# One attention wave for batch 0, the second product of block 0 by weight groups, spreads of four pairs and output stores on another queue

## The chip, the cores and the metric

The kernel runs on one core of one Trainium2 chip. The metric is the device time of a whole execution in microseconds (us). The profile's span, from the first to the last instruction, is about 2 us shorter than that time.

## The reference

```python
def _attn_ref(q, k, v):                       # B, H, S, D = 8, 8, 576, 64
    theta = np.pi / 2.0 * np.arange(S) / S
    phi = lambda x: concat([relu(x) * cos(theta), relu(x) * sin(theta)])
    q_p, k_p = phi(q), phi(k)
    kv = einsum('bhsf,bhsd->bhfd', k_p, v)
    z = sum(k_p, axis=2)
    return einsum(q_p, kv) / (einsum(q_p, z) + 1e-06)
# x = attention output as 4608 rows of 512; then, with w_in (512 x 2048) and w_out (2048 x 512)
def _moe_ref(x, w_in, w_out):
    h = x @ w_in
    return (h * sigmoid(1.702 * h)) @ w_out
```
The kernel keeps x in on-chip memory, transposed, and never writes it out.

## The kernel before

Nine blocks of 512 rows each go through the two products. Step n of a block is one chunk of the first product (`mm1`, steps 0 to 15) or a quarter of an output tile of the second (`mm2`, steps 16 to 31). The attention of batch i+1 is cut into small units that are laid between the steps of block i. Only batch 0's attention has nothing to hide behind.

```python
    def mm1(i, fc):                      # 4 products, then gelu on ACT into one of 18 buffers
        hps = hps_tile()                 # 2 PSUM buffers
        ...
        nc.scalar.activation(g, hps, AF.Gelu_apprx_sigmoid)
    def mm2(i, t, part):                 # 4 of the 16 products of output tile t
        if part == 0:
            cur[t] = yps_tile()          # 2 PSUM buffers
        ...
        if part == 3:
            ysb = ypool.tile([128, d_model], F32, name="ysb")     # 3 buffers
            nc.scalar.copy(ysb, yps)
            ...
            nc.scalar.dma_start(out=out[...], in_=ysb[...])       # stores issued by ACT
    # batch 0, before the blocks
    for jh in range(2):                  # the whole path twice, two pairs of heads each time
        ...                              # scale v (DVE, some on ACT)
        unit_kv(0, 2 * jh); unit_kv(0, 2 * jh + 1)
        unit_den(0, 2 * jh, 2 * jh + 2)  # denominators, reciprocal, split into three parts
        warmup(4)                        # products on a zero tile, results unused
        for j in (2 * jh, 2 * jh + 1):
            unit_spread(0, j)            # 4 small products (32 rows) and 2 ACT copies
            unit_num(0, j)               # numerator products, times spread, into x
    # between the steps of block i, for batch b = i + 1
    for j in range(NP):
        at(k0 + 22 + 2 * j, unit_spread, b, j)
        at(min(32, k0 + 23 + 2 * j), unit_num, b, j)
```

w_in is requested when batch 0's v has landed, batch 1 when w_in has, and w_out when batch 1's v has.

## Time and profile before

| | before |
|---|---|
| median time | 353.48 us (three runs when the prediction was made, 352.16 to 353.84) |
| span of the profile, mean granted clock | 350.0 us, 0.963 |
| TensorE busy | 326.8 us, 93% |
| VectorE (DVE), ScalarE (ACT) busy | 157.1 and 138.9 us |
| first w_in product of block 0 / block 1 / block 2 | 38.07 / 77.28 / 112.01 us |

The table of busy time by stage, in the prediction below, is the one to read: where TensorE does not keep up with its own work (block 0's start, and the 0.93 us at some block ends) something else sets the time. Everywhere else only fewer TensorE microseconds help.

### The profile page before, as it was taken

The numbers are of one execution on the slowest core, as the hardware profiler recorded it, in microseconds if no ns is written. First come the engines' busy times: TensorE is split into PE (matmuls) and PEld (weight loads), VectorE is DVE, ScalarE is ACT, GpSimd is POOL, SyncE is SP. The second block draws the span as 40 slices with busy tenths as digits, with TensorE's granted clock in tenths as the row PEclk, the third lists the DMA queues.
The fourth block names the chain that finished last, engine by engine and source line by source line (L and its number), as shares of the span: only waits on it lengthen the run. The fifth ranks groups of instructions, "written<-read, shape, count | busy, mean of one in ns | idle before, by whom it ended". The sixth has DMA issues, their size and how long they took to land.

```text
span 350.0 us, 4868 instructions
## 1 busy us (share of the span) xinstructions
PE 326.8 (93%) x1861; PEld 158.4 (45%) x1896; DVE 157.1 (45%) x388; ACT 138.9 (40%) x259; POOL 16.4 (5%) x45
## 2 busy tenths in 40 slices
PE   8477899999999899999998999999989999999994
PEld 3242345444544454445444544454535444444441
DVE  5657734447635644574457444654474420000000
ACT  3321553146322642264226423642364236424611
POOL 8400500000000000000000000000000000000000
PEclk9755899999999999999999999999999999999998
DMA  7999999913951893059215921501140120011022
GB/s 219 245 190 348 331 229 283 315 65 69 326 139 31 121 350 94 30 118 367 72 41 137 346 56 55 99 0 62 31 97 3 30 62 30 0 75 46 0 61 61
DMA packets 62217, 45.80 MB, mean 131 GB/s; under 512 B 28914, under 2 KB 57586, under 8 KB 62194
## 3 DMA queue, kind: packets, MB, share of 16 engines
q1 hardware_dynamic: 52466, 31.86, 32.1%
q10 hardware_dynamic: 5504, 9.44, 9.7%
q0 software_dynamic: 4224, 4.19, 7.3%
q8 instruction: 15, 0.25, 0.3%
q14 instruction: 8, 0.07, 0.1%
HBM read 36.70 MB, written 9.44 MB: 132 GB/s over the span
## 4 chain that ended last, share of the span: by engine, by line
PE 83%; DVE 9%; ACT 3%; ACTq 2%; issue 2%; DVEq 0%
PE hps L320 34%; PE yps L348 30%; PE at L259 5%; PE at L310 5%; PE at L298 3%; DVE den L285 3%; PE hps L72 2%; PE at L276 2%; ACTq L354 2%; PE att L208 1%; DVE vt L252 1%; ACT ysb L352 1%; DVE den L289 1%; DVE den L287 1%; DVE qT L212 1%
## 5 line engine op out<-in xcount | busy, mean ns | idle before, releaser
L348 PE MATMUL yps<-w_out_sb,g 128*128 128x512 bf16 x552 | 135.3, 380 | 1.7 <-issue 0.8
L320 PE MATMUL hps<-xT,w_in_sb 128*128 128x512 bf16 x566 | 129.4, 382 | 4.8 <-ACT g L323 4.1
L323 ACT ACTIVATE g<-hps 128x512 bf16<-128x512 f32 x144 | 85.5, 597 | 49.9 <-PE hps L320 49.5
L320 PEld LDWEIGHTS <-w_in_sb 128*128 128x128 bf16 x576 | 56.4, 98 | 72.3 <-issue 8.5
L348 PEld LDWEIGHTS <-g 128*128 128x128 bf16 x576 | 53.5, 98 | 54.5
L352 ACT COPY ysb<-yps 128x512 f32<-128x512 f32 x36 | 21.1, 586 | 77.1 <-PE yps L348 72.2
L312 DVE TENSOR_TENSOR xT<-at,invb 128x288 bf16<-128x288 f32 x64 | 26.7, 453 | 54.3 <-PE at L310 52.3
L302 ACT COPY invb<-at 128x288 f32<-128x288 f32 x64 | 22.6, 402 | 70.1 <-PE at L298 69.6
L262 DVE TENSOR_TENSOR zs<-at,mask_z 128x256 bf16<-128x256 f32 x32 | 13.6, 425 | 33.5 <-PE at L259 33.5
L259 PE MATMUL at<-vt,kr 128*128 128x258 bf16 x160 | 25.5, 289 | 2.7 <-DVE vt L252 1.3
L225 DVE TENSOR_TENSOR qT<-qTr,trig 128x576 bf16<-128x576 bf16 x48 | 18.2, 452 | 15.3 <-DMA qTr<-qn 15.3
L310 PE MATMUL at<-qT,kvs 128*128 128x288 bf16 x128 | 22.5, 297 | 0.7 <-ACT invb L302 0.5
L259 PEld LDWEIGHTS <-kr 128*128 128x128 bf16 x160 | 16.0, 101 | 13.3 <-issue 2.6
L252 DVE TENSOR_SCALAR vt<-vf,cosw 128x512 bf16<-128x512 f32 (+3 forms) x45 | 19.6, 447 | 0.0
L252 DVE TENSOR_SCALAR vt<-vf,sinw 128x512 bf16<-128x512 f32 (+3 forms) x39 | 18.1, 463 | 0.0
L298 PE MATMUL at<-den,sel 32*128 32x144 bf16 x128 | 14.1, 229 | 3.3 <-DVE den L289 3.1
L310 PEld LDWEIGHTS <-kvs 128*128 128x128 bf16 x128 | 12.6, 100 | 10.1 <-issue 1.4
L298 PEld LDWEIGHTS <-sel 32*128 32x128 bf16 x128 | 8.0, 94 | 17.9 <-issue 13.3
L265 DVE TENSOR_TENSOR kvs<-at,mask_n 128x256 bf16<-128x256 f32 x32 | 13.3, 414 | 0.0
L72 PE MATMUL hps<-warm 128*128 128x512 bf16 x31 | 11.3, 535 | 1.5 <-DVE halfpi L115 1.2
L212 DVE TENSOR_TENSOR qT<-att,trig 128x576 bf16<-128x576 bf16 x16 | 6.5, 450 | 9.3 <-PE att L208 9.3
L196 DVE TENSOR_SCALAR qn<-qf 128x1024 bf16<-128x1024 f32 x15 | 10.4, 696 | 0.0
(56 smaller groups left out, 95.9 us busy)
## 6 DMA issues: line engine op xcount, KB each, us to landing
qf<-in_q_dram SPq DMA_DIRECT2D x7, 1024.0 KB, 5.9
kf<-in_k_dram SPq DMA_DIRECT2D x7, 1024.0 KB, 8.4
vf<-in_v_dram SPq DMA_DIRECT2D x7, 1024.0 KB, 9.1
out_dram<-ysb ACTq DMA_DIRECT2D x40, 128.0 KB, 2.4
out_dram<-ysb ACTq DMA_DIRECT2D x16, 256.0 KB, 2.3
w_in_sb<-in_moe_w_in_dram POOLq DMA_DIRECT2D x4, 512.0 KB, 8.7
w_out_sb<-in_moe_w_out_dram POOLq DMA_DIRECT2D x4, 512.0 KB, 13.6
qf<-in_q_dram SPq DMA_DIRECT2D x2, 512.0 KB, 5.0
```

Source lines behind the costliest of these rows:

```text
L72: nc.tensor.matmul(wps, warm[:, 0:128], warm, start=True, stop=True)
L225: nc.vector.tensor_tensor(s["qT"][:, j, cs, :], s["qTr"][:, j, :], trig[:, cs, :], op=MUL)
L252: nc.vector.tensor_scalar(o, i, w, None, op0=MUL)
L259: nc.tensor.matmul(kv_ps[:, 0:VW], kr[:, c, j, :], vt[:, c, j, :], start=(c == 0), stop=(c == 4))
L298: nc.tensor.matmul(bps[:, ds(g2 * SEG, SEG)], sel[32 * j:32 * j + 32, 2 * hf + g2].rearrange("p hh d -> p (hh d)"), s["comb"][32 * j:32 * ...
L302: nc.scalar.copy(invb, bps[:, 0:HF])
L310: nc.tensor.matmul(num_ps[:, 0:HF], s["kvs"][j][:, cs, :], s["qT"][:, j, cs, ds(hf * HF, HF)], start=(cs == 0), stop=(cs == 1))
L312: nc.vector.tensor_tensor(xT[:, j, ds(b * S + hf * HF, HF)], num_ps[:, 0:HF], s["invb"][j, hf], op=MUL)
L320: nc.tensor.matmul(hps, w_in_sb[:, kc, ds(fc * 128, 128)], xT[:, kc, ds(i * TB, TB)], start=(kc == 0), stop=(kc == NP - 1))
L323: nc.scalar.activation(g, hps, AF.Gelu_apprx_sigmoid)
L348: nc.tensor.matmul(yps, gT[fc][:, ds(t * 128, 128)], w_out_sb[:, fc, :], start=(fc == 0), stop=(fc == FC - 1))
L352: nc.scalar.copy(ysb, yps)
```

## The change

The intent: run batch 0's attention path once instead of twice; hide late w_out groups; use four row groups of the array at once; take the stores off ACT.

```diff
-    SRC = (("qf", q), ("kf", k), ("vf", v))
+    SRC = (("qf", q), ("vf", v), ("kf", k))
 ...
-            cur[t] = yps_tile()
+            cur[t] = hps_tile() if i == 0 and t >= 2 else yps_tile()
 ...
-                nc.scalar.dma_start(out=out[...], in_=ysb[...])
+                nc.sync.dma_start(out=out[...], in_=ysb[...])
 ...
+    def unit_spread(b, hf):
+        bps = [at_tile() for _ in range(NP)]
+        for g2 in range(2):
+            for j in range(NP):
+                nc.tensor.matmul(bps[j][...], sel[32 * j:32 * j + 32, ...], s["comb"][32 * j:32 * j + 32, :], ...)
+        for j in range(NP):
+            nc.scalar.copy(invb, bps[j][:, 0:HF])
 ...
-    for jh in range(2):  ... (the two half waves)
+    warmup(14)
+    for j in range(NP):
+        unit_kv(0, j)
+    unit_den(0)
+    warmup(10)
+    for hf in range(2):
+        unit_spread(0, hf)
+        for j in range(NP):
+            unit_num(0, j, hf)
 ...
+            for hf in range(2):
+                n = k1 + 9 + 7 * hf
+                at(min(32, n), unit_spread, b, hf)
+                for j in range(NP):
+                    at(min(32, n + 3 + j // 2), unit_num, b, j, hf)
 ...
+            elif i == 0:
+                mm2(i, n % 4, (n - FC) // 4)
```
(Left out, among others: the attention's four PSUM buffers now serve transposes too, batch 0's kv results are copied by ACT, in blocks 1 to 6 the DMA transposes and the next loads are issued in the other order, the denominator has one more step before the spread, and w_in and w_out are asked for when the last load, now k, has landed.) In block 0 the loads of batch 2, called at step 28, now come on the SP queue behind the first output store, because both are on SP.

More of the change, by code (lines that the diff above doesn't have):

```diff
@@ L63, in yps_tile, with at_tile @@
         return ps.tile([128, TB], F32, name="yps", bufs=2)
-    def at_tile(dt=F32):
-        return ps.tile([128, TB if dt == F32 else 2 * TB], dt, name="at" if dt == F32 else "att",
-                       bufs=3 if dt == F32 else 1)
+    def at_tile():
+        return ps.tile([128, TB], F32, name="at", bufs=4)
     def warmup(n):
@@ L102 @@
     load_part(s0["qf"], q, 0, 4, 8)
+    load_part(s0["vf"], v, 0, 0, 8)
+    load_tail(s0["vf"], v, 0)
+    load_tail(s0["kf"], k, 0)
     load_part(s0["kf"], k, 0, 0, 4)
-    load_tail(s0["kf"], k, 0)
-    load_part(s0["vf"], v, 0, 0, 4)
-    load_tail(s0["vf"], v, 0)
     load_part(s0["kf"], k, 0, 4, 8)
-    load_part(s0["vf"], v, 0, 4, 8)
     tmp = ExitStack()
@@ L201, in prep_q_tail, with transpose_pe @@
                                 op0=MAX)
-    def transpose_pe(b, j):
+    def transpose_pe(b, j, step):
         s = state[b]
-        tp = at_tile(BF16)
-        for c in range(5):
-            np_ = 128 if c < 4 else 64
-            nc.tensor.transpose(tp[:, c * 128:c * 128 + np_],
-                                s["qn"][:np_, c, 2 * j:2 * j + 2, :].rearrange("p h d -> p (h d)"),
-                                ident[:np_, :np_])
+        if step == 0:
+            s["tp", j] = tp = at_tile().bitcast(BF16)
+            for c in range(5):
+                np_ = 128 if c < 4 else 64
+                nc.tensor.transpose(tp[:, c * 128:c * 128 + np_],
+                                    s["qn"][:np_, c, 2 * j:2 * j + 2, :].rearrange("p h d -> p (h d)"),
+                                    ident[:np_, :np_])
+            return
         for cs in range(2):
-            nc.vector.tensor_tensor(s["qT"][:, j, cs, :], tp[:, 0:S], trig[:, cs, :], op=MUL)
+            nc.vector.tensor_tensor(s["qT"][:, j, cs, :], s["tp", j][:, 0:S], trig[:, cs, :], op=MUL)
     def transpose_dma(b):
@@ L259, in unit_kv @@
             nc.tensor.matmul(kv_ps[:, 0:VW], kr[:, c, j, :], vt[:, c, j, :], start=(c == 0), stop=(c == 4))
-        kvs = two.tile([128, 2, 128], BF16, name="kvs", bufs=4)
+        if b == 0:
+            kvs = s["kvs0"][j]
+        else:
+            kvs = two.tile([128, 2, 128], BF16, name="kvs", bufs=4)
         zs = two.tile([128, 2, NSEG, 32], BF16, name="zs", bufs=4)
@@ L264, in unit_kv, with unit_den @@
             mask_z.rearrange("p s hh t r -> p s (hh t r)").unsqueeze(1).to_broadcast([128, 2, NSEG, 32]), op=MUL)
-        nc.vector.tensor_tensor(kvs, kv_ps[:, 0:256].rearrange("p (cs e) -> p cs e", cs=2), mask_n, op=MUL)
+        kv3 = kv_ps[:, 0:256].rearrange("p (cs e) -> p cs e", cs=2)
+        if b == 0:
+            for r in (slice(0, 64), slice(64, 128)):
+                nc.scalar.copy(kvs[r, :, r], kv3[r, :, r])
+        else:
+            nc.vector.tensor_tensor(kvs, kv3, mask_n, op=MUL)
         s.setdefault("kvs", []).append(kvs)
         s.setdefault("zs", []).append(zs)
-    def unit_den(b, j0=0, j1=NP):
+    def unit_den(b):
         s = state[b]
@@ L274, in unit_den @@
             for cs in range(2):
-                for j in range(j0, j1):
+                for j in range(NP):
                     nc.tensor.matmul(den_ps[32 * j:32 * j + 32, 0:SEG], s["zs"][j][:, cs, g, :],
@@ L278, in unit_den @@
                                      start=(g == 0 and cs == 0), stop=(g == NSEG - 1 and cs == 1))
-        r = slice(32 * j0, 32 * j1)
-        if j0 == 0:
-            s["d"] = [two.tile([128, SEG], dt, name=f"den{n}", bufs=1)
-                      for n, dt in enumerate((F32, F32, BF16, F32, BF16, BF16))]
-        den, inv, p0, d1, p1, comb = s["d"]
-        nc.vector.tensor_scalar(den[r], den_ps[r, 0:SEG], 1e-6, None, op0=ADD)
-        nc.vector.reciprocal(inv[r], den[r])
-        nc.vector.tensor_copy(p0[r], inv[r])
@@ L287, in unit_den @@
-        nc.vector.scalar_tensor_tensor(d1[r], p0[r], part1[r], inv[r], op0=MUL, op1=ADD)
-        nc.vector.tensor_copy(p1[r], d1[r])
-        nc.vector.scalar_tensor_tensor(comb[r], p1[r], part2[r], d1[r], op0=MUL, op1=ADD)
+        den, inv, p0, d1, p1, comb = [two.tile([128, SEG], dt, name=f"den{n}", bufs=1)
+                                      for n, dt in enumerate((F32, F32, BF16, F32, BF16, BF16))]
+        nc.vector.tensor_scalar(den, den_ps[:, 0:SEG], 1e-6, None, op0=ADD)
+        nc.vector.reciprocal(inv, den)
@@ L290, in unit_den @@
+        nc.vector.tensor_copy(p0, inv)
+        nc.vector.scalar_tensor_tensor(d1, p0, part1, inv, op0=MUL, op1=ADD)
+        nc.vector.tensor_copy(p1, d1)
+        nc.vector.scalar_tensor_tensor(comb, p1, part2, d1, op0=MUL, op1=ADD)
         s["comb"] = comb
-    def unit_spread(b, j, on=None):
+        s["invb"] = {}
+    def unit_spread(b, hf):
         s = state[b]
-        s.setdefault("invb", {})
-        for hf in range(2):
-            bps = at_tile()
-            for g2 in range(2):
-                nc.tensor.matmul(bps[:, ds(g2 * SEG, SEG)],
+        bps = [at_tile() for _ in range(NP)]
+        for g2 in range(2):
+            for j in range(NP):
+                nc.tensor.matmul(bps[j][:, ds(g2 * SEG, SEG)],
@@ L299, in unit_spread, with unit_num @@
                                  sel[32 * j:32 * j + 32, 2 * hf + g2].rearrange("p hh d -> p (hh d)"),
                                  s["comb"][32 * j:32 * j + 32, :], start=True, stop=True)
-            invb = two.tile([128, HF], F32, name="invb", bufs=4)
-            nc.scalar.copy(invb, bps[:, 0:HF])
+        for j in range(NP):
+            invb = two.tile([128, HF], F32, name="invb", bufs=8)
+            nc.scalar.copy(invb, bps[j][:, 0:HF])
             s["invb"][j, hf] = invb
-    def unit_num(b, j):
+    def unit_num(b, j, hf):
@@ L306, in unit_num @@
         s = state[b]
-        for hf in range(2):
-            num_ps = at_tile()
-            for cs in range(2):
-                nc.tensor.matmul(num_ps[:, 0:HF], s["kvs"][j][:, cs, :], s["qT"][:, j, cs, ds(hf * HF, HF)],
-                                 start=(cs == 0), stop=(cs == 1))
-            nc.vector.tensor_tensor(xT[:, j, ds(b * S + hf * HF, HF)], num_ps[:, 0:HF], s["invb"][j, hf], op=MUL)
-    gT = {}
+        num_ps = at_tile()
+        for cs in range(2):
+            nc.tensor.matmul(num_ps[:, 0:HF], s["kvs"][j][:, cs, :], s["qT"][:, j, cs, ds(hf * HF, HF)],
+                             start=(cs == 0), stop=(cs == 1))
@@ L317, in mm1, with mm1_part, gelu @@
+        nc.vector.tensor_tensor(xT[:, j, ds(b * S + hf * HF, HF)], num_ps[:, 0:HF], s["invb"][j, hf], op=MUL)
+    gT = {}
+    def mm1_part(hps, i, fc, kc):
+        nc.tensor.matmul(hps, w_in_sb[:, kc, ds(fc * 128, 128)], xT[:, kc, ds(i * TB, TB)],
+                         start=(kc == 0), stop=(kc == NP - 1))
+    def gelu(hps, fc):
+        g = gpool.tile([128, TB], BF16, name="g")
+        nc.scalar.activation(g, hps, AF.Gelu_apprx_sigmoid)
+        gT[fc] = g
     def mm1(i, fc):
@@ L319, in mm1 @@
         for kc in range(NP):
-            nc.tensor.matmul(hps, w_in_sb[:, kc, ds(fc * 128, 128)], xT[:, kc, ds(i * TB, TB)],
-                             start=(kc == 0), stop=(kc == NP - 1))
-        g = gpool.tile([128, TB], BF16, name="g")
-        nc.scalar.activation(g, hps, AF.Gelu_apprx_sigmoid)
-        gT[fc] = g
+            mm1_part(hps, i, fc, kc)
+        gelu(hps, fc)
     def pieces(m):
@@ L353, in mm2 @@
             for (p0, n, row, step) in pieces(i * 4 + t):
-                nc.scalar.dma_start(out=out[row:row + (n - 1) * step + 1:step, :], in_=ysb[p0:p0 + n, :])
+                nc.sync.dma_start(out=out[row:row + (n - 1) * step + 1:step, :], in_=ysb[p0:p0 + n, :])
     junk = const.tile([1, 16], F32)
     AC = nc.scalar
+    s0["kvs0"] = [two.tile([128, 2, 128], BF16, name="kvs", bufs=4) for _ in range(NP)]
+    for t in s0["kvs0"]:
+        nc.gpsimd.memset(t, 0.0)
     prep_new(0)
@@ L362 @@
     prep_q(0, 4, 8, AC)
-    warmup(24)
-    transpose_pe(0, 0)
-    transpose_pe(0, 1)
+    warmup(26)
+    for j in range(NP):
+        transpose_pe(0, j, 0)
+    for j in range(2):
+        transpose_pe(0, j, 1)
+    for c in range(5):
+        prep_v(0, c, 0)
+        prep_v(0, c, 1, on=AC)
+    for j in range(2, NP):
+        transpose_pe(0, j, 1)
     prep_k(0, 0, 4, AC)
     prep_k_tail(0)
-    transpose_pe(0, 2)
-    transpose_pe(0, 3)
-    nc.gpsimd.tensor_copy(junk[:, 0:1], s0["vf"][0:1, 0:1])
+    prep_k(0, 4, 8)
+    nc.gpsimd.tensor_copy(junk[:, 0:1], s0["kf"][0:1, 0:1])
     for g in range(4):
@@ L375 @@
     load_all(1)
-    nc.gpsimd.tensor_copy(junk[:, 1:2], state[1]["vf"][0:1, 0:1])
+    nc.gpsimd.tensor_copy(junk[:, 1:2], state[1]["kf"][0:1, 0:1])
     for g in range(4):
         nc.gpsimd.dma_start(out=w_out_sb[:, ts(g, 4), :], in_=wout_r[:, ts(g, 4), :])
-    for jh in range(2):
-        if jh == 1:
-            prep_k(0, 4, 8, AC)
-        for c in range(5):
-            prep_v(0, c, 0, 4 * jh, 4 * jh + 4)
-            prep_v(0, c, 1, 4 * jh, 4 * jh + 4, AC if c < 3 else None)
-        unit_kv(0, 2 * jh)
-        unit_kv(0, 2 * jh + 1)
-        unit_den(0, 2 * jh, 2 * jh + 2)
-        warmup(4)
-        for j in (2 * jh, 2 * jh + 1):
-            unit_spread(0, j)
-            unit_num(0, j)
+    warmup(14)
[5 more added lines that the diff above has]
+        unit_spread(0, hf)
+        for j in range(NP):
+            unit_num(0, j, hf)
     for i in range(NBLK):
@@ L401 @@
         if b < B:
-            if i > 0:
-                at(0, load_all, b + 1) if b + 1 < B else None
-            k0 = 4 if i == 0 else 0
+            k0 = 6 if i == 0 else 0
             at(k0, prep_new, b)
@@ L407 @@
             at(k0, prep_q_tail, b)
-            at(k0 + 1, prep_q, b, 4, 8)
+            at(k0, prep_q, b, 4, 8)
             if i == 0:
                 for j in range(NP):
-                    at(k0 + 5 + j, transpose_pe, b, j)
-            else:
-                at(k0 + 1, transpose_dma, b)
-            at(k0 + 2, prep_k, b, 0, 4)
-            at(k0 + 2, prep_k_tail, b)
-            at(k0 + 3, prep_k, b, 4, 8)
+                    at(k0 + 2 + j, transpose_pe, b, j, 0)
+                    at(k0 + 2 + j, transpose_pe, b, j, 1)
+            else:
+                at(k0, transpose_dma, b)
+                if b + 1 < B:
+                    at(k0 + 1, load_all, b + 1)
             for c in range(5):
                 for cs in range(2):
-                    at(k0 + 4 + c, prep_v, b, c, cs)
+                    at(k0 + 2 + c, prep_v, b, c, cs)
+            at(k0 + 7, prep_k, b, 0, 4)
+            at(k0 + 7, prep_k_tail, b)
+            at(k0 + 8, prep_k, b, 4, 8)
             if i > 0:
@@ L422 @@
                     at(k0 + 9 + j, prep_trig, b, j)
+            k1 = 17 if i == 0 else 12
             for j in range(NP):
-                at(k0 + 14 + j, unit_kv, b, j)
-            at(k0 + 19, unit_den, b)
-            for j in range(NP):
-                at(k0 + 22 + 2 * j, unit_spread, b, j)
-                at(min(32, k0 + 23 + 2 * j), unit_num, b, j)
+                at(k1 + j, unit_kv, b, j)
+            at(k1 + 5, unit_den, b)
+            for hf in range(2):
+                n = k1 + 9 + 7 * hf
+                at(min(32, n), unit_spread, b, hf)
+                for j in range(NP):
+                    at(min(32, n + 3 + j // 2), unit_num, b, j, hf)
             if i == 0 and b + 1 < B:
```

## The prediction

> **What bounds the kernel now.** I read the page's slices first, then busy time by stage, then the chain, then the order of time at the places where a stage ends.
>
> ```profile
> PE   8477899999999899999998999999989999999994
> ...
> PEclk9755899999999999999999999999999999999998
> ...
> DMA  7999999913951893059215921501140120011022
> ```
> (The page's slices, 8.75 us each.) TensorE is busy everywhere except in slices 2 to 4, where it also runs at half clock, while the DMA engines are full until about 70 us. So there are two regimes: a start limited by loads and by a serial chain, and a long stretch that is nothing but TensorE work.
>
> ```profile
> core 0: us, PE busy (x) PEld busy (x) DVE busy (x) ACT busy (x) POOL busy (x), PEclk, DMA share, GB/s
> ...
> 23.04:38.07 15.03, 11.73 (x63) 5.72 (x63) 9.17 (x25) 4.95 (x12) 0.17 (x2) 0.61 1.07 310
> 38.07:56.00 17.93, 17.29 (x82) 7.49 (x83) 11.12 (x25) 10.13 (x16) 4.73 (x5) 0.93 1.17 259
> 56.00:77.28 21.28, 20.73 (x147) 10.91 (x149) 8.11 (x21) 5.81 (x13) 0.00 (x0) 1.00 0.73 226
> 77.28:112.20 34.92, 34.43 (x211) 17.17 (x213) 20.78 (x51) 14.12 (x28) 0.00 (x0) 1.00 0.51 146
> 112.20:147.85 35.65, 34.33 (x209) 17.07 (x212) 18.92 (x47) 14.59 (x28) 0.00 (x0) 1.00 0.57 146
> ```
> (Busy time by stage; I cut at the first w_in product of each block.) Block 0 starts at 38.07 us. A steady block takes 34.7 to 35.9 us. No other engine has over 21 us of work in it. Blocks 1 to 6 sum to 211.6 us, blocks 7 and 8 take 27.8 and 28.55, the tail after the last product 4.8.
>
> ```profile
> 22.62 0.37 DVE den L289
> 23.04 0.63 PE at L298 x4
> ...
> 34.66 0.38 DVE den L289
> 35.08 0.41 PE at L298 x4
> ```
> (The chain of waits in order of time.) Batch 0's attention is run twice, for pairs 0-1 and for pairs 2-3: the same serial path (values, kv, denominator, reciprocal, spread, numerator) comes back 12.04 us later (35.08 - 23.04). That repetition is the largest thing to win.
>
> ```profile
> 112.21 0.59 ACT L352 COPY ysb<-yps 128x512 f32<-128x512 f32 x1 [2.35 <-PE yps L348]
> ...
> 112.83 1.34 ACTq L354 DMA_DIRECT2D out_dram<-ysb  x2
> ...
> 114.86 2.32 PE L320 MATMUL hps<-xT,w_in_sb 128*128 128x512 bf16 x10 [0.96 <-ACT g L323]
> ```
> (Order of time at a block's end.) ACT copies the last output tile, then spends 1.34 us issuing two stores, and only then does the first gelu; TensorE waits 0.96 us for a PSUM buffer.
>
> ```profile
> 172.63 1.03 PE L348 MATMUL yps<-w_out_sb,g 128*128 128x512 bf16 x4
> 173.59 0.42 PE L298 MATMUL at<-den,sel 32*128 32x144 bf16 x4
> 173.94 1.04 PE L348 MATMUL yps<-w_out_sb,g 128*128 128x512 bf16 x4
> 174.82 0.41 PE L310 MATMUL at<-qT,kvs 128*128 128x288 bf16 x2
> ```
> (TensorE alone in a steady block.) Four w_out products take 0.86 us (174.82 - 173.94 with a small switch). From 172.63 to 173.94 is 1.31, so one spread of four small products costs 1.31 - 0.86 = 0.45 us. They are about 0.06 us apart (0.24 in all); some 0.21 is entering and leaving the 32-row shape.
>
> **What the Trainium skill says.** "TensorE: Matmul & The Clock Gate", Part 1: the array runs at half clock after a mostly idle window of about 3.4 us and needs about as much dense work to get back. The trace agrees: 1.00 up to 13 us, 0.50 by 14 us after the thinly spaced transposes, and back only at about 32 us; it is 0.50 again when block 0 begins. "TensorEngine Tiling (Array Packing)", Overview, Key Properties: changing the tiling mode drains the array, and different tiles can load weights and multiply in parallel. The first agrees with the 0.21 us; before's spreads use one row group at a time, so nothing there shows the second. "Trainium Kernel Development and Optimization", Key Constraints: the SP, ACT and POOL queues share the same 16 DMA engines, and issuing elsewhere saves only issue time. Here that time is exactly what blocks the gelu.
>
> **The change, part by part.**
>
> *Loads and the single wave.* Before moved 2.91 MB by 12 us (summing 1 us stretches), and a load is seen by its user about 2 us after its bytes are counted. In the order q, v, k: v (2.23 MB cumulated) at 11.8 us, its tail at 12.2, first k half (3.01 MB) at 14.3, second (3.54 MB) at 15.9. Then:
> - DVE: two trig pairs to about 11.9, five cosine scalings at 0.40 to 14.0, two trig pairs (1.64) to 15.7, k tail 16.1, second k half (0.68) 16.8.
> - ACT: five sine scalings. A 256-wide one takes 0.43 and a 1024-wide relu 1.06, so 512 wide is about 0.64: 12.0 to 15.2; first k half 1.06 to 16.3.
> - TensorE: four kv at 0.55 from 16.3 to 18.6; last zs on DVE 19.1; denominator products 0.7 to 19.8; the six DVE steps take 2.7 as before (20.29 to 22.98) to 22.5.
> - Spread half 0: about 0.4, four ACT copies of 0.35 (1.4), last numerator 0.42, multiplication 0.45: to 25.2. Half 1 needs all four PSUM buffers back, so the path repeats: to about 27.9. Numerators lie before the first w_in product, whose fourth step alone needs the last pair: block 0 starts at about **27.4** us instead of 38.07, so -10.7.
>
> *Block 0.* First gelu with its table load (1.28 + 0.6) after the first product: third product at 27.4 + 2.85. Fourteen more at 0.865 = 12.1, four transposes 2.2: 44.55. w_out is requested once the last load of batch 1 is in: w_in is asked for about 2 us later (14.5 against 12.5), batch 1 about 1 us later (25.6 against 24.5), takes 13.4 as before, so 39.0; the first w_out group needs about 6 us (w_in's quickest landing was 6.1): 45.2. The others follow by about 2.55 us, while a round over four tiles eats 3.5 us: only the first group can be waited for, about 0.8. I add 0.4 for a lapse of the clock: 45.75. Sixteen steps 13.85, kv 2.2, denominator 0.93, first spread 0.6, four numerators 0.98: 64.3. The second spread and its numerators lie bare at the end: spread 0.45, ACT 1.5, numerator 0.42, DVE 0.47, less what the first product may do before pair 3, about 2.3: block 1 starts at **66.6**, not 77.28. So block 0 itself goes from 39.2 to 39.2.
>
> *Spreads of four.* Eight products with four row groups replace two spreads: streams of 0.12 (all parallel) to 0.48 (serial), plus one switch 0.21. Weight loads were about 0.045 us apart, so eight take 0.36 even when products overlap: I take 0.6 each. Per batch 4 x 0.45 - 2 x 0.6 = 0.6 us; six blocks: -3.6.
>
> *More room after the denominator.* Four steps (3.46 us) instead of three lie beside the DVE chain; a wait of about 0.15 goes in each of six blocks: -0.9.
>
> *Stores on SP.* The waits of TensorE for gelu total 4.1 us in five cases; the first, 0.55, is the table load. The other four, at the ends of blocks 1, 3, 5 and 7, go: -3.5.
>
> So blocks 1 to 6: 211.6 - 3.6 - 0.9 - 2.6 = 204.5 (including small rearrangements), plus 0.5 for a late batch 2 in block 1; block 8 27.7. Sum 66.6 + 205 + 27.8 + 27.7 + 4.8 = 331.9 us of span. The profiled run was 2.15 us longer than its span and the median 3.5: **334 us**, 5.5% less.
>
> **The rivals.**
> 1. *The clock lapses in the wave.* For: half clock held from 14 to 32 us although TensorE looked 70 to 90% busy. Against: 14 and 10 warming products fill the gaps that I find after the transposes and beside the reciprocal. If it lapses before the denominator, the ten warming products take 4.3 instead of 2.2 and delay the spread by about 2, numerators and first products lose 2 more: 338.
> 2. *Transfers take over.* w_out late by 4 us or more would give back that much. For: DMA is full up to 70 us. Against: in before, batch 2 was loaded right alongside w_out; now the load sits behind the first store of block 0 in SP's order. The price is that batch 2 is asked for only at about 61 us, for use from 67 us on; its k lands at about 75, the DMA transposes come behind it, and DVE's zs then end about when the denominator wants them. 335 to 339 if this bites.
> 3. *The spreads really run in parallel*: 0.33 each, 1.1 saved per batch: 330.
> 4. *Stores on SP wait behind loads*, and the three output buffers run out. Against: loads need 7.5 us of issue after 6.5 of transposes, finishing before the first store's turn at about 19 us of a block. Under 1 us.
>
> **Range and chances.** Start +-2, clock up to +4, w_out and batch 2 up to +4, spreads -3 to +1: 328 to 341. To lose 2% threshold (346.4) nearly all the 10.7 us must come back, so faster 0.97.
>
> **What would show it.** Block 0's first w_in product at 26 to 30 us at clock 1.00; no wait at block ends for gelu; eight spread products within 0.5 to 0.7; steady blocks at 34.0; mm2's wait for w_out under 1.5 us. I am wrong if the wave ends after 31 us, if the clock is 0.50 in it, or if block 1 exceeds 36 us because batch 2 was asked for late.

## The result and the profile after

The changed kernel takes 332.33 us (median of four runs, 331.8 to 334.4). The kernel before takes 352.86 in the same rounds. The ratio is 0.9411, with a 95% interval of 0.9352 to 0.9471. Ratios are the mean time of one kernel's runs over that of the other's of the same rounds, so not quite the ratio of the medians quoted; they count a fifth run of the changed kernel too, of 329.89 us. The forecast of 334 holds, but its parts do not all hold.

The page's slices of the changed kernel (8.3 us each):

```profile
PE   8887989899799999999999999999999999999994
...
PEclk9999999999899999999999999999999999999999
...
DMA  7799796497952494139433961394230220021022
```
The half-clock valley of slices 2 to 4 is gone. Two weaker TensorE slices remain (the 7s, near 29 and 87 us), and the DMA row, solid up to 70 us before, has a hole in the eighth slice.

Busy time by stage, cut again at first w_in products (the columns are those shown for before):

```profile
22.45:27.23 4.78, 3.56 (x33) 2.12 (x34) 2.19 (x6) 2.62 (x8) 0.00 (x0) 1.00 1.24 207
27.23:44.68 17.45, 16.18 (x84) 7.52 (x84) 10.02 (x24) 10.13 (x16) 3.27 (x5) 1.00 0.81 227
44.68:67.48 22.80, 19.50 (x147) 10.33 (x148) 9.54 (x24) 5.46 (x13) 0.00 (x0) 1.00 0.70 138
67.48:105.07 37.59, 35.52 (x211) 17.23 (x213) 18.54 (x47) 14.51 (x28) 0.00 (x0) 0.95 0.77 217
...
172.38:205.56 33.18, 32.86 (x210) 16.53 (x212) 18.64 (x47) 14.51 (x28) 0.00 (x0) 1.00 0.56 157
```
Block 0 starts at 27.23 us instead of 38.07. It takes 40.25 us (39.21 before), of which 3.3 us idle in its second product (22.80 against 19.50 busy). Block 1 takes 37.59 (34.73 before). A steady block takes 33.18.

The wave in order of time:

```profile
16.05 2.38 PE L259 MATMUL at<-vt,kr 128*128 128x258 bf16 x20 [1.50 <-ACT kr L231]
...
22.45 0.30 PE L303 MATMUL at<-den,sel 32*128 32x144 bf16 x8 [0.57 <-DVE den L294]
```
There is one path through kv, denominator and reciprocal instead of two 12 us apart, and in this run all of it at full clock. (The spread comes in two halves, the second 2 us later.) The forecast had kv at 16.3, the spread at 22.5 and block 0 at 27.4.

Block 0's end (columns: start, duration, engine and line, operation; in brackets the idle time before it and what ended it):

```profile
61.61 0.36 SPq L365 DMA_DIRECT2D out_dram<-ysb  x1
...
62.07 0.38 SPq L76 DMA_DIRECT2D qf<-in_q_dram  x1
...
65.39 0.59 ACT L363 COPY ysb<-hps 128x512 f32<-128x512 f32 x1 [1.60 <-DMA out_dram<-ysb]
65.88 1.31 ACT L308 COPY invb<-at 128x288 f32<-128x288 f32 x4
66.33 1.31 PE L315 MATMUL at<-qT,kvs 128*128 128x288 bf16 x8 [1.57 <-ACT invb L308]
```
Batch 2's loads were issued only at 62 us, behind the first output store. The fourth output copy waited for an output buffer whose store was slow to land. The spread's copies stand behind that one on ACT, and TensorE stands behind them.

Block 1, further on in the same order of time:

```profile
73.62 7.73 SPq L219 DMA_TRANSPOSE qTr<-qn  x5
...
82.57 3.04 DVE L225 TENSOR_TENSOR qT<-qTr,trig 128x576 bf16<-128x576 bf16 x8 [4.22 <-DMA qTr<-qn]
...
87.98 0.68 PE L284 MATMUL at<-qT,zs 128*32 128x144 bf16 x29 [0.42 <-DVE zs L265]
...
88.99 4.91 PE L359 MATMUL yps<-w_out_sb,g 128*128 128x512 bf16 x15 [0.33 <-issue]
```
The transposes of q start late, so DVE's zs end late and the denominator waits. After that pause TensorE runs at half clock: 4.91 us for 15 products that take about 3.4 in a steady block.

A steady block, TensorE alone:

```profile
199.06 2.75 PE L359 MATMUL yps<-w_out_sb,g 128*128 128x512 bf16 x11
201.75 0.30 PE L303 MATMUL at<-den,sel 32*128 32x144 bf16 x8
201.99 1.25 PE L359 MATMUL yps<-w_out_sb,g 128*128 128x512 bf16 x5
```
Eight spread products now take 0.24 us of TensorE's order (201.99 - 201.75), plus about 0.11 for the changes of shape, nearly all of it on entering: the first spread product starts 0.31 us after the last wide one, where wide ones follow each other by 0.22. Before, four took 0.45 in all.

### The profile page after: what moved, and what is told of

It is laid out like the page before. It is cut to its first block, busy times and chain, and to the rows that moved or that the text cites. A ratio compares the mean times of both kernels' runs of the same rounds, so it can differ in the third digit from the quotient of the medians.

```text
span 332.3 us, 4902 instructions
## 1 busy us (share of the span) xinstructions
PE 313.9 (94%) x1880; PEld 153.8 (46%) x1914; DVE 149.5 (45%) x370; ACT 139.3 (42%) x265; POOL 16.4 (5%) x49
## 4 chain that ended last, share of the span: by engine, by line
PE 78%; issue 8%; DMA 6%; SPq 4%; DVE 2%; POOL 1%; ACT 1%; POOLq 0%; ACTq 0%; DVEq 0%
PE yps L359 35%; PE hps L323 31%; PE at L259 4%; PE at L315 4%; DMA kf<-in_k_dram 2%; SPq L219 2%; DMA w_out_sb<-in_moe_w_out_dram 2%; PE hps L359 2%; PE at L284 1%; SPq L81 1%; POOL w_in_sb L393 1%; DMA out_dram<-ysb 1%; PE at L303 1%; DVE qT L225 1%; DMA qTr<-qn 1%
## 5 line engine op out<-in xcount | busy, mean ns | idle before, releaser
L359 PE MATMUL yps<-w_out_sb,g 128*128 128x512 bf16 x529 | 124.3, 383 | 3.3 <-DMA w_out_sb<-in_moe_w_out_dram 1.6
L259 PE MATMUL at<-vt,kr 128*128 128x258 bf16 x160 | 22.3, 273 | 1.5 <-ACT kr L231 1.5
L315 PE MATMUL at<-qT,kvs 128*128 128x288 bf16 x128 | 19.9, 285 | 2.5 <-ACT invb L308 2.5
L252 DVE TENSOR_SCALAR vt<-vf,cosw 128x512 bf16<-128x512 f32 (+1 forms) x40 | 19.0, 483 | 2.0 <-DMA vf<-in_v_dram 1.9
L252 DVE TENSOR_SCALAR vt<-vf,sinw 128x512 bf16<-128x512 f32 (+1 forms) x35 | 16.9, 484 | 0.0
L71 PE MATMUL hps<-warm 128*128 128x512 bf16 x49 | 13.8, 444 | 1.3 <-DVE halfpi L113 1.2
L273 DVE TENSOR_TENSOR kvs<-at,mask_n 128x256 bf16<-128x256 f32 x28 | 11.6, 412 | 0.0
L233 DVE TENSOR_SCALAR kr<-kf 128x1024 bf16<-128x1024 f32 x15 | 10.2, 679 | 0.0
L71 PEld LDWEIGHTS <-warm 128*128 128x128 bf16 x50 | 5.2, 110 | 8.6 <-issue 3.6
L290 DVE RECIPROCAL den<-den 128x144 f32<-128x144 f32 x8 | 8.4, 1053 | 0.3
```

The source lines that it names most:

```text
L71: nc.tensor.matmul(wps, warm[:, 0:128], warm, start=True, stop=True)
L252: nc.vector.tensor_scalar(o, i, w, None, op0=MUL)
L259: nc.tensor.matmul(kv_ps[:, 0:VW], kr[:, c, j, :], vt[:, c, j, :], start=(c == 0), stop=(c == 4))
L315: nc.tensor.matmul(num_ps[:, 0:HF], s["kvs"][j][:, cs, :], s["qT"][:, j, cs, ds(hf * HF, HF)], start=(cs == 0), stop=(cs == 1))
L359: nc.tensor.matmul(yps, gT[fc][:, ds(t * 128, 128)], w_out_sb[:, fc, :], start=(fc == 0), stop=(fc == FC - 1))
```

## The experiments

Twelve kernels ran, in three calls. The calls ran on different chips, so the changed kernel ran twice more as a yardstick, in the first call (with e1 to e3) and in the third (with e4, e6 and e11). The second call (e5, e8, e9, e10) has none; its totals are set against the yardsticks of the others, which a difference between chips could blur. This table is read off the traces: the time of block 0's first w_in product, then how long the blocks took from first product to first product, then what follows (from spans rounded to 0.1 us).

| run | start | block 0 | block 1 | blocks 2-6 | block 7 | rest | median time |
|---|---|---|---|---|---|---|---|
| before | 38.07 | 39.21 | 34.73 | 176.70 | 27.74 | 33.55 | 352.86 |
| after | 27.23 | 40.25 | 37.59 | 166.87 | 27.63 | 32.73 | 332.33 |
| a0_after_again | 26.94 | 40.42 | 35.37 | 166.88 | 27.63 | 32.66 | 332.01 |
| e1_gate | 29.36 | 43.58 | 34.10 | 166.88 | 27.63 | 32.65 | 336.50 |
| e2_serial | 29.77 | 39.58 | 34.92 | 166.98 | 27.63 | 32.72 | 331.79 |
| e3_nowarm | 29.90 | 38.25 | 35.32 | 166.88 | 27.63 | 32.72 | 333.00 |
| e5_mm2_order | 28.28 | 43.67 | 33.72 | 166.88 | 27.62 | 32.73 | 334.95 |
| e8_wave_alone | 33.29 | 46.65 | 34.74 | 176.42 | 27.74 | 33.66 | 355.97 |
| e9_gate_4buf | 27.59 | 39.19 | 33.76 | 168.49 | 27.93 | 32.94 | 332.16 |
| e10_best | 30.59 | 37.54 | 33.71 | 167.51 | 27.92 | 32.93 | 332.13 |
| a1_after_third | 28.68 | 39.72 | 34.82 | 166.88 | 27.63 | 32.67 | 332.75 |
| e4_act_stores | 29.55 | 44.80 | 33.55 | 166.88 | 27.63 | 33.59 | 339.50 |
| e6_k_first | 31.86 | 38.65 | 34.48 | 166.88 | 27.63 | 32.70 | 335.00 |
| e11_best18 | 31.31 | 36.91 | 33.50 | 166.45 | 27.63 | 32.90 | 330.81 |

Three things help in reading it. The start moves by almost 2 us between runs of the very same kernel, mostly because batch 0's loads land earlier or later (the scaling of v began at 11.81, 10.81 and 13.27 us in the three runs; the start came 15.42, 16.13 and 15.41 us after it). The clock adds to that.

The warming products end at a time that q sets, kv (the products of k with v) begins at a time that v sets, and between them TensorE idles. In the three runs of the changed kernel and in e5_mm2_order this gap was 0.44 to 1.56 us, in e9_gate_4buf 2.38, and kv ran at full clock (2.37 us). In e1_gate, e4_act_stores, e2_serial, e10_best and e11_best18 it was 2.12 to 3.49 us, the granted clock fell to one half before or during kv, and kv took 3.64 to 4.04 us. None of these edits but the last two's early table load comes before kv, so their starts of 29.4 to 31.3 us are not shown to be an effect of the edits.

And part of a late start comes back in block 0, which waits for w_out in any case.

**a0_after_again and a1_after_third: the changed kernel, unedited.**

> The changed kernel once more, as the yardstick of this call. Both theories: about 332.3 us, ratio about 0.941 to the kernel before; block 0's first w_in product at 27.2 us, block 1 at 67.5 us, block 2 at 105.1 us, blocks 4 to 6 at 33.2 us each.

> The changed kernel as the yardstick of this call: 331 to 333 us, first w_in product 27 to 29.5 us as the first loads come, block 0 40.3 us, block 1 35 to 38, later blocks 33.7, 33.6, 33.2.

Measured: 332.01 and 332.75 us, ratios 0.9391 (0.9352 to 0.9430) and 0.9433 (0.9380 to 0.9486). Block 1 took 35.37 and 34.82, so of the 37.59 in the first profile some 2 us were a half-clock episode that not every run has. The late denominator is in all three traces. The run profiled for the result above was the slowest of its five, 334.4 us.

**e1_gate: batch 2's loads as soon as w_out has landed, no longer behind the first store.**

```diff
-                at(28, load_all, b + 1)
+                at(16, gate_w_out)       # SP: a 4-byte copy that reads the last w_out group
+                at(16, load_all, b + 1)
```

> Batch 2's loads no longer behind block 0's first store on SP; they are issued when w_out has landed (about 54 us instead of 62). Theory A (the late batch 2 causes block 1's loss: q-transposes at 73.6 us, denominator held by DVE until 88, then half clock): block 1 falls from 37.6 to 33.7 us, and the bare end of block 0 loses about 1 us because the output stores no longer stand behind the loads; total 4 to 5 us less, about 327.5. Rival B (block 1 is slow because DMA transposes and loads share engines wherever they lie, or the clock lapses by itself): block 1 stays over 36 us and the total within 1 us of the changed kernel.

Measured: 336.5 us, slower. Block 1 did fall, to 34.10, as theory A says. But block 0 rose to 43.58, with TensorE at half clock from 67.84 us on. In order of time:

```profile
64.75 6.32 SPq L365 DMA_DIRECT2D out_dram<-ysb  x4
...
70.13 0.59 ACT L363 COPY ysb<-hps 128x512 f32<-128x512 f32 x1 [5.82 <-DMA out_dram<-ysb]
...
71.07 2.08 PE L315 MATMUL at<-qT,kvs 128*128 128x288 bf16 x8 [5.79 <-ACT invb L308]
```
Now all four stores stand behind the six loads on SP. The first could be issued at 64.75 us only, although its copy was made at 61.5, and the fourth copy waited 5.82 us for one of three output buffers. The expectation of 1 us less at block 0's end was wrong: I had moved the collision, not removed it. This is rival 4 of the prediction, at the one place where I had not looked.

The traces say more about block 1 than this run alone. Its length follows the time at which batch 2's last q transpose lands, counted from the block's first product: 12.78, 13.55, 13.90, 14.39 and 14.44 us in e5_mm2_order, e6_k_first, a1, e3_nowarm and a0 go with blocks of 33.72, 34.48, 34.82, 35.32 and 35.37, one for one. In e5_mm2_order the loads were asked for as late as in the changed kernel (5.3 us before the block, 5.4 there), and block 1 lost nothing; only one store, not three, lay between those loads and the transposes on SP. So it is the landing of the transposes, not of the loads as such, that sets block 1's length in these traces.

**e9_gate_4buf: the same with a fourth output buffer.**

```diff
+ (e1_gate)
-    gpool ... bufs=18      ypool ... bufs=3
+    gpool ... bufs=17      ypool ... bufs=4
```

> As e1_gate (batch 2 loaded as soon as w_out has landed), with four output buffers instead of three (and 17 instead of 18 gelu buffers to make room). Theory A (e1_gate was slower only because the four stores of block 0 stood behind the loads and the fourth copy waited 5.8 us for a buffer): that wait is gone, block 0 takes 38.5 to 39.5 us, block 1 33.7 to 34.2, total 327 to 329. Rival B (loads earlier hurt in another way): block 0 stays over 41 us.

Measured: 332.16 us; block 0 39.19 and block 1 33.76, both as theory A has them, though its total of 327 to 329 was missed. The line that waited before now reads:

```profile
64.69 0.59 ACT L363 COPY ysb<-hps 128x512 f32<-128x512 f32 x1 [0.77 <-PE hps L359]
```
The copy waits for its products only. The total is nevertheless no better than the yardsticks, because the blocks from 2 on became slower: 168.49 for 166.88, and block 7, which has no attention in it, 27.93 for 27.63. 17 gelu buffers in place of 18 were the suspect. At the end of block 0 TensorE now waits 0.74 us where it waited 1.57, so the missing buffer had cost it 0.8.

**e10_best and e11_best18: three more changes, and the 18th gelu buffer back.**

```diff
+ (e9_gate_4buf)
+    nc.scalar.activation(junk_g, halfpi, AF.Gelu_apprx_sigmoid)   # load the gelu table early
-    nc.gpsimd.tensor_copy(junk[:, 1:2], state[1]["kf"][0:1, 0:1])
+    nc.gpsimd.tensor_copy(junk[:, 1:2], state[1]["vf"][0:1, 0:1]) # ask for w_out one load earlier
-                n = k1 + 9 + 7 * hf
+                n = k1 + 9 + 6 * hf
  e11 alone: gpool back to 18, invb 8 -> 7 buffers
```

> e9_gate_4buf and three more: w_out asked for when batch 1's v has landed (not k), the gelu table loaded at the start by a one-element activation, the second spread one step earlier. Theory A: the w_out wait (1.6 us) and the table wait (1.2 us) go, the waits at the starts of blocks 1 to 3 (0.45 each) go: 3 to 4 us under e9_gate_4buf, about 324. Rival B (k of batch 1 is late, or relu and copies reload a table): no gain or a second table load in the profile.

> e10_best with the 18 gelu buffers kept (room from 7 instead of 8 spread buffers). Theory A (the 17th buffer was worth 0.2 us in every block: e9_gate_4buf and e10_best took 33.4 in steady blocks and 27.9 in block 7 for 33.2 and 27.6): steady blocks return to 33.2 and block 7 to 27.6, block 0 37.5 to 38, block 1 33.7; total 4 to 6 us under the yardstick, about 326 to 328. Rival B (the steady blocks were slower because of the chip): they stay at 33.4 and the total is within 2 us of the yardstick.

Measured: e10 332.13 us; e11 330.81, against 332.75 for the changed kernel in the same call (ratios to before 0.9364, 0.9322 to 0.9406, and 0.9433; the intervals overlap). Block by block theory A holds: block 0 37.54 and 36.91, block 1 33.71 and 33.50, blocks 2 and 3 of e11 33.44 each for 33.68 and 33.63. Steady blocks return to 33.19 and block 7 to 27.63 with the 18th buffer, so that buffer was worth about 0.2 us in a steady block and 0.3 in block 7. The forecast totals were missed: e10's 324, set on e9_gate_4buf's own forecast, by 8 us, and e11's 326 to 328 by 3. The start has a large part in both, 30.59 and 31.31 us. Against e9_gate_4buf's 27.59, v came 1.4 and 1.1 us later, and the rest of the delay is mostly half clock at kv, behind gaps of 3.43 and 3.49 us; in e11 the clock lapsed once more at 29.71. The first half of k also came later, 3.2 and 3.5 us after v against 2.0 to 2.7 in the other kernels that load v first, but that moved kv by 0.1 and 0.4 us only (4.34 and 4.63 us after v, for 4.24). Both have the early table load in common; whether it delays k, or two late draws fell together, is open. e11 has the lowest median of all that ran, 1.9 us under the yardstick of its call and 1.0 under e2_serial, the next; by its interval it is not clear of the changed kernel.

**e2_serial: the eight spread products in pair order.**

```diff
-        for g2 in range(2):
-            for j in range(NP):
+        for j in range(NP):
+            for g2 in range(2):
```

> The eight spread products in pair order (the two of one row group one after the other) instead of going round the four row groups. Theory A (the products of different row groups run side by side, 0.24 us for eight in the changed kernel): a spread becomes 0.35 to 0.5 us, 14 of them in batches 1 to 7, total 1.5 to 3.5 us more, steady blocks 33.4 to 33.7. Rival B (the gain came from entering the 32-row shape twice a batch instead of four times): a spread stays at 0.24 us, no change.

Measured: 331.79 us; the spread takes 0.31 instead of 0.30 us:

```profile
193.63 0.31 PE L303 MATMUL at<-den,sel 32*128 32x144 bf16 x8
193.88 2.76 PE L359 MATMUL yps<-w_out_sb,g 128*128 128x512 bf16 x12
```
The time is rival B's, but B's reason does not suffice. Entering the narrow shape half as often cannot make eight products take less (0.24 us from the first to the next wide product) than four of one row group took before (0.35). At before's spacing of 0.063 us eight in a row would need 0.5. So products of different row groups do overlap, and they do so in either order. (This rests on the total of eight; which product overlaps which, the recorded starts do not show. No run puts the old spreads back.) In batch 0's wave, where nothing hides the path, the pair order was even quicker: 4.13 us from the first spread product to block 0's start, for 4.77 in the changed kernel. Theory A was right that they overlap and wrong that the order brings it about.

**e3_nowarm: without the 14 and 10 warming products.**

> Without the 14 and 10 warming products of batch 0's wave. Theory A (they hold the clock): the granted clock in 16 to 27 us falls to 0.5, kv takes 4.3 us for 2.2, numerators and the first w_in products run at half speed; block 0's first product at 29 to 30 instead of 27.2 us. Because w_out is not there before 46.2 us anyway, 1.6 us of this is hidden behind that wait: total +1 to +3. Rival B (the wave hangs on DVE, ACT and DMA, the clock is of no matter): first product by 27.8 us, total within 0.5.

Measured: 333.0 us, 1.0 more than the yardstick of its call (the means differ by 1.8; the intervals of the ratios overlap). By three-microsecond windows:

```profile
16.00:19.00 3.00, 3.00 (x16) 2.15 (x15) 1.04 (x3) 1.04 (x4) 1.23 (x2) 0.53 1.13 171
...
25.00:28.00 3.00, 2.42 (x15) 1.14 (x14) 1.83 (x4) 0.82 (x4) 0.00 (x0) 0.50 1.05 182
```
The granted clock (third from the right) is 0.53 and 0.50 where the profiled changed kernel has 1.00 in both windows. The start is 29.90 though v was there at 11.34, so 18.56 us after v instead of 15.42. Block 0 gives 2 us of it back. Theory A holds, at the low end. The warming products are no guarantee, either. In e1_gate and e4_act_stores, which have them, kv ran at half clock all the same, and the start came 17.07 us after v. So they bring 3.1 us where they hold the clock and 1.5 where they do not.

**e5_mm2_order: block 0's second product tile by tile.**

```diff
-            cur[t] = hps_tile() if i == 0 and t >= 2 else yps_tile()
+            cur[t] = yps_tile()
-            elif i == 0:
-                mm2(i, n % 4, (n - FC) // 4)
```

> Block 0's second product tile by tile again (each output tile needs all four w_out groups within 3.5 us of its start), all else as changed. The groups land about 46.2, 48.8, 51.4 and 54.0 us. Theory A (going by groups is what lets the second product begin at 46.3): the first tile ends near 55 instead of 51.5, block 0 gets about 3 us longer before its end, of which about 1.4 come back because the output stores are spread out and no copy waits for an output buffer; total +1 to +3, and TensorE shows waits for w_out of 4 to 6 us in place of 1.6. Rival B (w_out is there in time anyway): waits stay under 2 us and the total does not rise.

Measured: 334.95 us, 2.2 to 2.9 more than the yardsticks. The waits, in total and longest:

```profile
PE yps L359 <- DMA w_out_sb<-in_moe_w_out_dram: 5.3, 4, 2.3
```
In the changed kernel this line says 1.6 us, once. Block 0 takes 43.67 us and block 1 33.72. The four groups land 5.9 to 11.9 us after their request, much as in the changed kernel (5.6 to 11.6); going by tiles meets each of them with a wait. The group order is worth 2 to 3 us, as theory A had it.

**e8_wave_alone: the kernel before with the single wave and nothing else.**

```diff
 (on the kernel before)
-    load order q, k/2, v/2, k/2, v/2
+    load order q, v, k/2, k/2
-    for jh in range(2): ...
+    warmup(14); unit_kv x4; unit_den(0); warmup(10); then spread and numerator pair by pair
```

> The kernel before with nothing but batch 0 in one wave (loads q, v, k; shared work; 26, 14 and 10 warming products); spreads pair by pair, second product tile by tile and stores on ACT stay. Theory A (the wave's gain cannot pass w_out: it is asked for at about 40 us with batch 2's loads running beside it and lands at 59 to 61 us): first w_in product at 28 to 30 us, then TensorE waits about 10 us for w_out in block 0, block 1 starts at 76 to 78, total 350 to 354, next to nothing gained. Rival B (parts add up): block 1 starts at 67 to 68, total 343.

Measured: 355.97 us, ratio 1.0053 (1.0006 to 1.0100): nothing gained. The start is earlier by 4.8 us only (33.29; the kernel before has one PSUM buffer for transposes, so the fourth transpose waits for DVE, behind the v scalings, until 16.13 us; the 14 warming products behind it take 4.80 us at half clock and hold kv back to 21.48 us, for 16.05 in the changed kernel; spreads and numerators pair by pair then take 5.1 us, from 28.20, for 4.8). Block 0 then takes 46.65 us:

```profile
53.80 1.02 PE L347 MATMUL yps<-w_out_sb,g 128*128 128x512 bf16 x4 [1.73 <-DMA w_out_sb<-in_moe_w_out_dram]
58.13 1.86 PE L347 MATMUL yps<-w_out_sb,g 128*128 128x512 bf16 x4 [3.31 <-DMA w_out_sb<-in_moe_w_out_dram]
```
w_out lands 9.0 to 19.5 us after its request, because batch 2's loads run beside it. In the changed kernel it takes 5.6 to 11.6. The earlier start is worth something only together with the parts that keep the wait for w_out short. The size of the wait that I expected (10 us, measured 5.8 in three places) was off because the start came 4 us later than I thought.

**e4_act_stores: the output stores back on ACT.**

```diff
-                nc.sync.dma_start(out=out[...], in_=ysb[...])
+                nc.scalar.dma_start(out=out[...], in_=ysb[...])
```

> Output stores back on ACT, all else as changed. Theory A (the stores on SP free the gelus at block ends, but also, by accident, hold batch 2's loads back): the 0.93 us waits for gelu return at the ends of blocks 1, 3, 5 and 7 (+3.7); batch 2's loads run alongside w_out, whose first group lands 3 to 4 us later, so TensorE's wait for w_out grows from 1.6 to about 5 us; in exchange block 0's end loses its wait for an output buffer (-1.4) and block 1 its late denominator (-2 to -4). Sum +1 to +4. Rival B (which engine issues the stores is of no account beyond the gelu): +3.7 with w_out's wait unchanged. Rival C: no change at all.

Measured: 339.5 us, 6.75 more than the yardstick. The loss is not where my account of the stores had it. The end of block 5:

```profile
240.61 1.14 PE L315 MATMUL at<-qT,kvs 128*128 128x288 bf16 x8
240.81 0.59 ACT L363 COPY ysb<-yps 128x512 f32<-128x512 f32 x1 [0.66 <-PE yps L359]
...
241.43 1.12 ACTq L365 DMA_DIRECT2D out_dram<-ysb  x2
241.59 3.62 PE L323 MATMUL hps<-xT,w_in_sb 128*128 128x512 bf16 x16
```
ACT copies and issues two stores just as before, and TensorE does not wait. Eight numerator products (0.98 us) now lie between the last w_out product and the next block's first w_in product, and ACT's work fits beside them. Blocks 1 to 7 are no slower than with the stores on SP; only block 8, before which there is no attention, waits 0.76 us for gelu. The loss is in block 0, 44.80 us for 39.72 (the start, 0.9 later, had kv at half clock; block 1 gives 1.3 back):

```profile
50.41 2.98 PE L359 MATMUL yps<-w_out_sb,g 128*128 128x512 bf16 x8 [3.40 <-DMA w_out_sb<-in_moe_w_out_dram]
```
With no store ahead of them batch 2's loads go out from 35.66 us on, w_out lands 9.3 to 19.0 us after its request (5.8 to 12.0 in the yardstick), TensorE waits 3.40 us (1.12), then runs at half clock from 51.04 to 54.45. At the end of block 0 it waits 2.66 us (1.53) for the copies and store issues that crowd ACT. So of the 5.1 us in block 0 some 4 belong to the late w_out (2.3 for the wait, an estimated 1.7 for 3.4 us at half clock) and 1.1 to ACT. Theory A's second half is right and its first half wrong. Its sum of +1 to +4 was too small.

**e6_k_first: batch 0 in the order q, k, v, work unchanged.**

> Batch 0 loaded in the order q, k, v with the order of work (v first, then k) left as it is. Theory A (v first lets ten scalings run while k is still on its way): the scalings begin about 4 us later and so does the first w_in product, 31 us instead of 27 to 28; 1.6 us of it is hidden behind w_out, total +2 to +3. Rival B (the last load bounds the wave in either order): no change in the first product's time.

Measured: 335.0 us, 2.25 more than the yardstick (the means differ by 1.35, and the intervals overlap, so the total alone does not decide). The start is 31.86 for 28.68, and there is no wait for w_out left (1.1 us in the yardstick). But theory A's reason accounts for only part of it. The first profile of the changed kernel is the one to compare, since q landed at the same time there (8.42 and 8.38 us): v's scaling began 2.5 us later (14.34 for 11.81), not 4. The start came 4.6 us later, and the other 2.1 us lie in products at half clock (kv 1.4, those after the spread 0.7). The warming products had ended long before kv began:

```profile
18.58 3.76 PE L259 MATMUL at<-vt,kr 128*128 128x258 bf16 x20 [4.50 <-ACT kr L231]
```
The changed kernel has 2.38 us and a gap of 1.50 on this line. That the gap of 4.50 us brought the lapse fits the gaps told above, but no run separates it. Theory A's direction is right; its 31 us were met partly by luck.

## Why the prediction was right

Its time was right because the largest step was right and three wrong steps cancelled. Forecast against the spans of the profiled run (334.4 us): start 27.4 and 27.23; block 0 39.2 and 40.25; block 1 34.6 (34.1 and the 0.5 for a late batch 2) and 37.59; blocks 2 to 6 5 x 34.1 = 170.5 and 166.87; block 7 27.8 and 27.63; the rest 32.5 and 32.73. The deviations, -0.2 + 1.1 + 3.0 - 3.6 - 0.2 + 0.2, sum to +0.3. That the sum is so near is luck: this was the slowest of five runs, with a half-clock episode of some 2 us in block 1. In a0 and a1, without it, the sums are -2.1 and -1.6. One of the prediction's own signs of being wrong did appear, block 1 over 36 us because batch 2 was asked for late, in this run but not in the other two (35.37 and 34.82).

*Loads and the single wave.* Right step by step, within 0.3 us in the profiled run; the other two runs started at 26.9 and 28.7. It rests on two things. e3_nowarm shows the clock's part; e6_k_first shows 2.5 us for v first, with a lapse of the clock beside it. Rival 1, the lapse, did come true at kv in five of the ten traces that have v first and the warming products in the changed kernel's wave, and made kv 1.3 to 1.7 us longer each time. The prediction's reading of the clock in the kernel before is off in two places: it is back at full speed at 33.8 us and not 32, and the 1.00 of the first microseconds only means that no change was recorded yet, since the warming products follow each other by 0.427 us until 6.3 us and by 0.216 from 6.8 on. The cause "one path instead of two" is shown by the trace; e8_wave_alone shows that it pays only where the wait for w_out stays short. The prediction had this in rival 2, but as a danger and not as a condition.

*Block 0.* The wait for the first w_out group was seen, 0.8 us forecast and 1.6 measured (1.1 in another run), because w_out was requested at 40.6 and not 39.0. The gelu's table load cost more as well: the third product came 3.36 us after the first, not 2.85. What I missed is the output buffer: the fourth copy waits 1.6 us for a store that shares its queue with batch 2's loads. e9_gate_4buf removes it, and TensorE's wait falls by 0.8 us. Rival 4 said under 1 us, but from steady blocks; that the figure fits block 0 is luck, as e1_gate's 5.8 us shows.

*Spreads of four.* The mechanism was right, the size off: 0.6 us per spread of four pairs was the mis-sized term. It is 0.24 plus 0.11 for the changes of shape, so rival 3 (0.33) was the better figure. The step that was wrong is the weight loads: 0.36 us was set down for eight, and the trace has all eight within 0.12. That is 1.1 us saved per batch instead of 0.6, or 2.5 us of the 3.6 by which blocks 2 to 6 beat the forecast. The other 1.1 us stay open. e2_serial adds that the order of the products is of no account in a steady block.

*More room after the denominator.* Right: the waits of 0.15 us for DVE before a spread, one in each of blocks 1 to 6 of the kernel before, are gone in all six.

*Stores on SP.* This step failed. I wrote that the waits for gelu at the ends of blocks 1, 3, 5 and 7 go because the stores leave ACT, 3.5 us. e4_act_stores shows that three of the four go anyway, through the numerators that now lie there; the stores themselves are worth 0.75 us at block 8. What moving them did bring, about 5 us in block 0, came mostly (some 4 us) from something else: on SP the first store holds batch 2's loads back until w_out is through. The prediction saw that order, and counted it only as a rival's price.

*Late batch 2.* The 0.5 us were too little. In the three traces block 1 lost 1.1 to 3.8 us against e9_gate_4buf's 33.76, through the late transposes and, in the profiled run, the clock after the pause.

## What to carry to other kernels

A queue is an order as well as a path: moving a store to another queue changes what the loads behind it compete with, and that can be worth more than the issue time saved. Shortening a start-up is worth nothing until the next thing that lands late has been moved as well, so trial such parts together and alone. Idle time between warming products and the work that they warm for can undo them: here kv ran at half clock after most gaps of over 2 us. And read a total that fits with suspicion: only the stage table showed that three wrong terms had cancelled.

## What the Trainium skill lacked or had wrong

- "Trainium Kernel Development and Optimization", Key Constraints, says that issuing DMAs from several engines only saves issue time. Here the same stores issued by ACT and not by SP cost 6.75 us (339.5 against 332.75). Some 4 us of that (estimated in e4_act_stores above) come from order: on SP the first store holds 3.5 MB of loads back, on ACT it does not, and w_out's last group lands 19.0 and not 12.0 us after its request. The section does not say that a store which waits in a queue holds back what stands behind it.
- "TensorEngine Tiling (Array Packing)", Tiling Modes, Key Properties (the prediction names the right item under the wrong heading, Overview): that tiles multiply in parallel is borne out (eight products of four row groups in 0.24 us, where four of one group took 0.35). What it lacks is that the order of issue is of no account for the products themselves (0.30 and 0.31 us in the two orders).
- "TensorE: Matmul & The Clock Gate", the table "Why this matters for your kernels", asks for no idle gaps over about 3 us. In e1_gate and e4_act_stores gaps of 2.12 and 2.17 us were followed by kv products at half clock (4.04 us for 2.38); in e9_gate_4buf one of 2.38 us was not. So here a gap under 3 us was not always safe, and its length alone did not decide.
- No page has what one gelu buffer was worth in a kernel like this: 17 instead of 18 cost 0.2 us in a steady block and 0.3 in block 7 (e10_best against e11_best18).
